# A decayed attention and gated convolution kernel on one core: its list of all engines' work, searched anew from cross4 on

## The chip, the cores and the metric

The kernel runs on one core of a Trainium2 chip. The metric is the device time of one execution in microseconds; of the kernel before three executions took 216.40, 216.54 and 216.66 us, so its time is the median, 216.54 us. Lower is better.

## What is computed

Two stages run one after the other on float32 data: a causal attention with a decay per head, in blocks of 64 positions with a running state, and then a gate from a convolution of five taps that multiplies a projected value, followed by an output projection.

```python
for b in range(nb):                      # 12 blocks of 64 positions, 4 batches, 8 heads of 64
    intra = (qb @ kb.T * Dmask) @ vb     # "scores", "mask", "cross"/"own"
    inter = (qb * lam_pow) @ kv_state    # "scale_q", "inter"
    out[:, :, sl] = intra + inter
    kv_state = lam_block * kv_state + (kb * rev_pow).T @ vb   # "scale_k", "outer", "update"
x = out.transpose(0, 2, 1, 3).reshape(4, 768, 512)
gate_pre = sum(conv_w[k] * x_padded[:, k:k + S] for k in range(5))   # "tap0" to "tap4"
gate = 1 / (1 + exp(-gate_pre))          # "sigmoid"
val = x @ w_val                          # "value"
return (gate * val) @ w_out              # "apply", "split_h", "project", "evict", "store"
```

The inputs w_val, conv_w and w_out arrive as float64 and are taken apart into float32 in the first 30 us; this part is not touched by the change.

## The kernel before, in words

The twelve blocks are the unit of work, i = 0 to 11. For each block the plan in `decay_attention_then_gated_conv` adds named steps, each of one engine. On TensorE a block has six kinds: `scores` (64 small matmuls of 64x64 blocks, line 469), `outer` (64, line 500), `cross` and `own` (32 each, line 535), `inter` (64, line 548), then two `value-i-u-` (24 matmuls of 128x128 with 256 columns, line 722) and two `project-i-b` (12 matmuls with 512 columns, line 789; the last block's second half is cut in two). Every matmul is a pair of instructions, a weight load and the multiplication. The first five kinds use the array as four blocks of 64x64 and are called small here; `value` and `project` use all of it and are called large.

VectorE has `mask`, `update`, `tap1` to `tap4` (line 659), `apply`, and `split_x_lo` of blocks 0, 5, 8, 11. ScalarE has `tap0`, `sigmoid`, `change`, `keep`, `split_x` (lines 602 and 606), `split_h`, `evict` (line 797) and the `scale_k` of eight blocks. GpSimd has `scale_q` (two a block, line 446), the other `scale_k`, `split_x_lo` (line 617) and `split_h_lo` (line 766). SyncE's queue issues all loads `ld` (q and k as four DMAs under `ldi-q0`; `ldi-v` and `ldi-k` two each; 256 KB a DMA, line 333) and all 25 stores (line 800), in the order in which they are named.

Numbers count as follows: `value-i-0-` and `value-i-2-` are the halves of block i; `apply`, `split_h` and `split_h_lo` count on over halves, so that numbers 2i and 2i+1 are those of block i; `scale_q` has none for block 0 and two for each block after it, so scale_q20 and scale_q21 are those of block 11.

What runs when is set by the list ORDER (line 39) alone: 600 names. `Plan.run` walks through it and issues each step's instructions, so each engine's queue is the list's names of that engine in the list's order. An engine takes its queue strictly in order and waits at the first step whose inputs or buffers are not there. Buffers come from SLOTS: three for the loads of a block (`ld`), two banks of PSUM for `scores`, `outer` and the accumulator of `cross`, `own` and `inter` (`d`), three for `value` and `project` (`u`), one for the taps (`acc`), two for outgoing rows (`o`). The code checks that the list respects dependencies and that a buffer is free when it is taken; the numbers of nanoseconds beside each step are not used when the list is walked.

Of the kernel before, what the change touches and what calls it, by code (L numbers as in the profile page):

```python
# [36 lines left out]


ORDER = """
qdec0 dmask0 go0 parts1 float_low1 mask_m1 add_low1 go1 parts2 relu1 sign1 scale1 mask_m2 ld0-q0 relu2  # L40
float_low2 add_low2 scores0 sign2 scale2 high1 mask0 low1 high0 low0 ld0-q1 scores1 mask1 ld1-q0 scores2
scale_q0 ld0-k scale_k0 ld0-v cross0 load_conv0 change0 mask2 parts0 go2 parts3 relu0 sign0 go3 mask_m3 parts4
float_low0 relu3 sign3 float_low3 add_low3 scale_q1 history0 mask_m0 mask_m4 add_low0 outer0 update0 own0
split_x0 scale3 ld1-v cross1 split_x_lo0 change1 own1 high2 low2 relu4 sign4 inter0 value-0-2 ld1-k keep0 go5
parts6 float_low4 scale0 ld2-q0 scores3 keep1 tap0-0-0 scale_q2 scale_q3 scale_k1 outer1 ld2-v add_low4 mask_m6
value-0-0 scale4 high3 split_x1 low3 value-0-3 ld2-k ld3-q0 history1 split_x_lo1 relu6 tap1-0-0 tap2-0-0
tap3-0-0 scale_q4 mask3 tap4-0-0 sigmoid-0-0 update1 value-0-1 tap0-0-1 tap1-0-1 scale_q5 float_low6 float_m0
go4 tap2-0-1 tap3-0-1 tap4-0-1 scores4 mask4 sigmoid-0-1 apply0 cross2 value-1-0 tap0-0-2 tap1-0-2 change2 own2
ld4-k add_low6 scale_k2 parts5 relu5 ld3-k float_low5 ld3-v tap2-0-2 sign6 value-1-1 mask_m5 inter1 keep2
split_x2 split_x_lo2 scale6 tap3-0-2 add_low5 high5 tap4-0-2 sigmoid-0-2 outer2 value-1-2 low5 update2 cross3  # L50
change3 tap0-0-3 ld5-q0 value-1-3 own3 tap1-0-3 inter2 apply2 keep3 tap2-0-3 tap3-0-3 scale_k3 sign5 value-2-0-
split_h2 tap4-0-3 sigmoid-0-3 scale5 split_h_lo2 high4 tap0-1-3 apply3 split_h3 outer3 low4 ld4-q0 scores5 ld7-v
apply1 mask5 value-2-2- split_h_lo3 split_h1 tap1-1-3 scores6 tap2-1-3 tap3-1-3 tap4-1-3 split_h0 mask6 scale_k4
sigmoid-1-3 tap0-1-0 project-1-1 evict-1-1 update3 split_h_lo1 split_h_lo0 ld4-v ld5-v cross4 scale_q6 outer4
ld5-k split_x3 change4 tap1-1-0 tap2-1-0 tap3-1-0 project-0-1 tap4-1-0 scale_q7 scale_q8 update4 sigmoid-1-0
inter3 own4 ld7-k history2 split_x_lo3 tap0-1-1 evict-0-1 store-0-1 cross5 scale_q9 tap1-1-1 tap2-1-1 tap3-1-1
tap4-1-1 change5 sigmoid-1-1 apply4 tap0-1-2 project-1-0 evict-1-0 tap1-1-2 tap2-1-2 own5 ld6-v store-1-0 inter4
keep5 split_x5 tap3-1-2 ld6-q0 tap4-1-2 sigmoid-1-2 apply5 ld7-q0 keep4 value-3-2- apply7 tap0-2-2 tap1-2-2
tap2-2-2 scale_k5 split_h4 split_h_lo4 scale_q10 value-3-0- apply6 scale_q11 split_h5 split_h_lo5 tap3-2-2
scale_k7 tap4-2-2 sigmoid-2-2 project-0-0 split_x_lo5 tap0-2-1 tap1-2-1 ld6-k history3 scores7 outer5 mask7  # L60
update5 split_h6 split_h_lo6 split_h7 project-2-0 evict-2-0 split_x4 split_x_lo4 tap2-2-1 project-2-1 ld8-q0
cross6 store-1-1 evict-0-0 tap3-2-1 tap4-2-1 sigmoid-2-1 store-0-0 store-2-0 scores8 mask8 evict-2-1 change6
store-2-1 tap0-2-3 tap1-2-3 scale_k6 tap2-2-3 scale_q12 scale_q13 value-5-2- value-4-2- ld8-k tap3-2-3 scale_k8
split_h_lo7 project-3-1 outer6 inter5 tap4-2-3 sigmoid-2-3 apply9 own6 split_h9 update6 tap0-2-0 value-4-0-
apply11 tap1-2-0 tap2-2-0 tap3-2-0 scale_q14 scale_q15 tap4-2-0 project-3-0 keep6 ld10-q0 sigmoid-2-0 evict-3-1
cross7 change7 apply8 split_h8 split_h_lo8 split_h_lo9 split_x6 outer7 split_h11 split_h_lo11 own7 inter6
value-5-0- keep7 ld9-k tap0-3-1 scale_k9 ld8-v store-3-1 tap1-3-1 tap2-3-1 ld9-q0 tap3-3-1 tap4-3-1 sigmoid-3-1
scores9 apply10 tap0-3-0 mask9 project-4-1 evict-4-1 store-4-1 split_x_lo6 update7 tap1-3-0 tap2-3-0 tap3-3-0
tap4-3-0 evict-3-0 split_h10 ld10-v store-3-0 sigmoid-3-0 split_x7 tap0-3-2 tap1-3-2 value-6-2- cross8 scores10
split_h_lo10 scale_q16 project-5-0 history4 evict-5-0 mask10 tap2-3-2 tap3-3-2 change8 value-6-0- apply12  # L70
tap4-3-2 sigmoid-3-2 inter7 own8 outer8 project-4-0 tap0-3-3 tap1-3-3 update8 tap2-3-3 split_x_lo7 ld9-v ld10-k
value-7-2- cross9 split_x8 split_x_lo8 keep8 scores11 change9 own9 tap3-3-3 tap4-3-3 sigmoid-3-3 split_h12
apply13 split_h13 ld11-q0 scale_q17 store-5-0 scale_q18 inter8 keep9 tap0-4-1 tap1-4-1 evict-4-0 store-4-0
tap2-4-1 project-5-1 apply15 tap3-4-1 mask11 evict-5-1 tap4-4-1 store-5-1 value-7-0- sigmoid-4-1 outer9 split_x9
apply14 split_h14 cross10 change10 split_h15 history5 split_h_lo12 split_h_lo13 scale_q19 project-6-1 evict-6-1
store-6-1 tap0-4-2 update9 value-8-0- tap1-4-2 tap2-4-2 tap3-4-2 scale_q20 scale_k10 split_h_lo15 split_h_lo14
project-7-0 evict-7-0 project-7-1 tap4-4-2 sigmoid-4-2 inter9 tap0-4-0 ld11-v store-7-0 evict-7-1 tap1-4-0
tap2-4-0 tap3-4-0 outer10 update10 split_x_lo9 value-9-0- tap4-4-0 sigmoid-4-0 apply16 apply18 tap0-4-3
scale_q21 tap1-4-3 value-8-2- scores12 project-6-0 tap2-4-3 tap3-4-3 value-9-2- mask12 tap4-4-3 split_h18
store-7-1 sigmoid-4-3 split_h16 split_h_lo16 apply17 split_h_lo18 split_h17 cross11 change11 own10 keep10  # L80
inter10 own11 evict-6-0 store-6-0 split_h_lo17 keep11 tap2-5-3 tap0-5-1 apply19 tap1-5-1 project-8-0 project-8-1
split_h19 split_h_lo19 tap1-5-3 project-9-0 tap2-5-1 tap3-5-1 tap4-5-1 split_x11 split_x_lo11 split_x10
sigmoid-5-1 evict-8-1 evict-8-0 tap0-5-0 tap1-5-0 tap0-5-3 tap2-5-0 tap3-5-0 tap4-5-0 sigmoid-5-0 store-8-0
tap0-5-2 tap1-5-2 evict-9-0 tap3-5-3 split_x_lo10 join1-5-3 join2-5-3 join3-5-3 value-11-2- value-11-0-
store-8-1 store-9-0 tap2-5-2 tap3-5-2 tap4-5-3 join4-5-3 project-9-1 apply22 split_h22 evict-9-1 value-10-2-
value-10-0- split_h_lo22 tap4-5-2 sigmoid-5-3 sigmoid-5-2 apply23 split_h23 split_h_lo23 apply21 project-11-1-1
split_h21 split_h_lo21 apply20 split_h20 store-9-1 evict-11-1-1 split_h_lo20 project-11-0 evict-11-0 store-11-0
project-10-1 evict-10-1 store-11-1-1 store-10-1 project-10-0 project-11-1-0 evict-10-0 store-10-0 evict-11-1-0
store-11-1-0
""".split()  # L90


# [760 lines left out]
```

## Time and profile before

| | us |
|---|---|
| three executions | 216.40, 216.54, 216.66 |
| the profiled execution, its own time | 218.14 |
| its span, first to last instruction | 216.4 |
| TensorE busy in the span | 199.0 |
| VectorE, ScalarE, GpSimd busy | 143.5, 114.1, 101.6 |

The profiled execution took 218.14 us, of which 216.4 us lie between its first and last instruction; without the profiler the whole execution takes 216.54 us. A gap on TensorE that the profile puts down to "issue" is one in which no semaphore that the profile shows was waited for. The rows that the prediction uses stand in the section before it.

### The profile page before, as it was taken

The numbers are of one execution on the slowest core, as the hardware profiler recorded it, in microseconds if no ns is written. First come the engines' busy times: TensorE is split into PE (matmuls) and PEld (weight loads), VectorE is DVE, ScalarE is ACT, GpSimd is POOL, SyncE is SP. The second block draws the span as 40 slices with busy tenths as digits, with TensorE's granted clock in tenths as the row PEclk, the third lists the DMA queues.
The fourth block names the chain that finished last, engine by engine and source line by source line (L and its number), as shares of the span: only waits on it lengthen the run. The fifth ranks groups of instructions, "written<-read, shape, count | busy, mean of one in ns | idle before, by whom it ended". The sixth has DMA issues, their size and how long they took to land.

```text
span 216.4 us, 8533 instructions
## 1 busy us (share of the span) xinstructions
PE 199.0 (92%) x3832; PEld 175.1 (81%) x3832; DVE 143.5 (66%) x220; ACT 114.1 (53%) x193; POOL 101.6 (47%) x81
## 2 busy tenths in 40 slices
PE   8838659999997899999799998999999999999993
PEld 3437659999986698798689988899889998899983
DVE  2998998999999649725923956919448832774100
ACT  3326876886853394237437642363741239855221
POOL 1171469155999209690409175018650052655600
PEclk9976978999999999999999999999999999999999
DMA  6999999157681396734155991612141001211022
GB/s 228 352 386 387 384 353 306 53 151 245 204 286 53 101 289 252 220 123 145 37 162 164 314 301 59 177 72 100 53 138 57 5 0 55 85 60 48 3 103 91
DMA packets 19188, 35.70 MB, mean 165 GB/s; under 512 B 2384, under 2 KB 2640, under 8 KB 19152
## 3 DMA queue, kind: packets, MB, share of 16 engines
q1 hardware_dynamic: 19008, 35.16, 47.9%
q8 instruction: 30, 0.49, 1.0%
q14 instruction: 6, 0.05, 0.1%
q10 hardware_dynamic: 144, 0.00, 0.0%
HBM read 28.86 MB, written 6.29 MB: 162 GB/s over the span
## 4 chain that ended last, share of the span: by engine, by line
PE 83%; DMA 7%; DVE 6%; issue 3%; SPq 1%; ACT 0%; DVEq 0%; ACTq 0%
PE op L789 32%; PE vp L722 31%; PE xp L535 5%; PE st L500 5%; PE xp L548 5%; PE s L469 4%; DMA w_raw<-in_w_out 3%; DMA w_raw<-in_w_val 2%; DMA lam_bc<-in_lam 2%; DVE w_m L276 1%; DVE w_e L267 1%; DVE w_m L250 1%; DVE w_m L283 1%; DVE w_e L244 1%; SPq L364 1%
## 5 line engine op out<-in xcount | busy, mean ns | idle before, releaser
L659 DVE SCALAR_TENSOR_TENSOR acc<-x,conv_sb,acc 128x512 f32<-128x512 f32 x92 | 69.3, 753 | 31.4 <-ACT acc L654 29.5
L789 PE MATMUL op<-wo_hi,hs 128*128 128x512 f32 (+1 forms) x200 | 61.2, 388 | 0.3 <-issue 0.3
L722 PE MATMUL vp<-x_hi,wv_hi 128*128 128x256 f32 x192 | 55.1, 287 | 0.0
L766 POOL TENSOR_TENSOR hs<-g,hs 128x512 fp32r<-128x512 f32 x24 | 31.4, 1326 | 48.8 <-ACT hs L763 48.8
L722 PE MATMUL vp<-x_lo,wv_hi 128*128 128x256 f32 x192 | 53.7, 280 | 0.0
L722 PE MATMUL vp<-x_hi,wv_lo 128*128 128x256 f32 x192 | 53.6, 279 | 0.0
L789 PEld LDWEIGHTS op<-wo_hi,hs 128*128 128x128 f32 x200 | 35.7, 188 | 7.2
L446 POOL TENSOR_TENSOR qd<-ld,qdec 128x512 f32<-128x512 f32 x22 | 29.0, 1335 | 24.9 <-DMA ld<-in_qkv 15.9
L789 PE MATMUL op<-wo_lo,hs 128*128 128x512 f32 (+1 forms) x100 | 38.4, 384 | 0.0
L722 PEld LDWEIGHTS vp<-x_hi,wv_hi 128*128 128x128 f32 x192 | 36.5, 190 | 1.3
L722 PEld LDWEIGHTS vp<-x_lo,wv_hi 128*128 128x128 f32 x192 | 36.4, 190 | 0.3
L722 PEld LDWEIGHTS vp<-x_hi,wv_lo 128*128 128x128 f32 x192 | 36.5, 190 | 0.0
L676 ACT ACTIVATE g<-acc 128x512 f32<-128x512 f32 x23 | 13.7, 598 | 29.3 <-DVE acc L659 29.3
L735 DVE TENSOR_TENSOR g<-vp,g 128x512 f32<-128x512 f32 x24 | 16.2, 687 | 18.1 <-ACT g L676 12.4
L797 ACT COPY o<-op 128x512 f32<-128x512 f32 (+1 forms) x25 | 14.0, 569 | 25.7 <-PE op L789 19.8
L617 POOL TENSOR_TENSOR x_lo<-x,x_hi 128x1024 fp32r<-128x1024 f32 x8 | 19.9, 2493 | 11.3 <-ACT x_hi L606 8.4
L789 PEld LDWEIGHTS op<-wo_lo,hs 128*128 128x128 f32 x100 | 18.8, 188 | 4.2 <-issue 0.5
L535 PE MATMUL xp<-A,ld 64*64 64x64 f32 x768 | 17.2, 228 | 4.9 <-issue 3.1
L535 PEld LDWEIGHTS xp<-A,ld 64*64 64x64 f32 x768 | 14.4, 141 | 7.8 <-issue 4.8
L763 ACT CAST hs<-g 128x512 fp32r<-128x512 f32 x24 | 14.3, 617 | 6.7 <-DVE g L735 6.3
L500 PE MATMUL st<-ld 64*64 64x64 f32 x704 | 14.8, 236 | 3.0 <-ACT wv_hi L288 2.2
L469 PE MATMUL s<-ld 64*64 64x64 f32 x768 | 14.6, 228 | 3.2 <-DVE A L477 3.2
(56 smaller groups left out, 229.9 us busy)
## 6 DMA issues: line engine op xcount, KB each, us to landing
ld<-in_qkv SPq DMA_DIRECT2D x90, 256.0 KB, 5.3
out<-o SPq DMA_DIRECT2D x23, 256.0 KB, 2.1
w_raw<-in_w_out SPq DMA_DIRECT2D x8, 256.0 KB, 5.9
w_raw<-in_w_val SPq DMA_DIRECT2D x2, 512.0 KB, 3.9
ld<-in_qkv SPq DMA_DIRECT2D x2, 512.0 KB, 6.6
w_raw<-in_w_val SPq DMA_DIRECT2D x4, 256.0 KB, 4.8
out<-o SPq DMA_DIRECT2D x2, 128.0 KB, 1.9
conv_raw<-in_conv_w SPq DMA_DIRECT2D x1, 20.0 KB, 4.9
```

The lines of the kernel that those rows point to most:

```text
L446: nc.gpsimd.tensor_tensor(out=s["qd"][:, p], in0=lds[i]["qT"][:, p], in1=qdec[:, :, p][:, :, None, :].to_broadcast([P, 2, NB, L]), op=ALU. ...
L469: nc.tensor.matmul(s["s", n][half(a), z, p, b], kT[half(z), p, a, b], qT[half(z), p, a, b], start=True, stop=True, skip_group_check=True,)
L500: nc.tensor.matmul(s["st"][half(z), a, p, b], k_[half(a), p, z, b], v_[half(a), p, z, b], start=True, stop=True, skip_group_check=True,)
L535: nc.tensor.matmul(s["xp"][half(p), z, a, b], lds[i]["v"][half(a), p, z, b], s["A"][half(a), z, p, b], start=t == 1 and b == 0, stop=True, ...
L617: nc.gpsimd.tensor_tensor(out=s["x_lo"].rearrange("q g b i -> q (g b) i"), in0=s["x"].rearrange("q g b i -> q (g b) i"), in1=hi.rearrange( ...
L659: nc.vector.scalar_tensor_tensor(out=to, in0=source(kk), scalar=w, in1=to, op0=ALU.mult, op1=ALU.add)
L722: nc.tensor.matmul(s["vp", u][:, f, :], w[:, ct, fs], xx[:, ct, :], start=n_mm == 0, stop=n_mm == 3 * NT - 1,)
L735: nc.vector.tensor_tensor(out=gs(u), in0=val, in1=gs(u), op=ALU.mult)
L763: nc.scalar.copy(s["h_hi"][:, us], gs(u))
L766: (nc.vector if i in H_DVE else nc.gpsimd).tensor_tensor(out=s["h_lo"][:, us], in0=gs(u), in1=s["h_hi"][:, us].bitcast(F32), op=ALU.subtract,)
L789: nc.tensor.matmul(op[:, cols], hh[:, ft, ts], w[:, ft, cols], start=n_mm == 0, stop=n_mm == 3 * NT - 1,)
L797: nc.scalar.copy(s["o", b, j][:, cols], s["op", b, j][:, cols])
```

## The change

Only the string ORDER differs. Its text is broken into lines anew, so that the diff shows all of it, but the first 205 names (up to `ld4-v ld5-v tap1-1-0`) are the same and stand in the same order. From there on the other 395 names stand in a new order; none is added or removed, and no other line of the kernel changes. The search that made the new list counted the semaphore waits of TensorE among the instructions of its program packets, and had the loads land later; neither figure is in the kernel.

The old list from `cross4` on (its first eleven lines), and the new one in full from the line in which it departs:

```diff
 ORDER = """
...
-sigmoid-1-3 tap0-1-0 project-1-1 evict-1-1 update3 split_h_lo1 split_h_lo0 ld4-v ld5-v cross4 scale_q6 outer4
-ld5-k split_x3 change4 tap1-1-0 tap2-1-0 tap3-1-0 project-0-1 tap4-1-0 scale_q7 scale_q8 update4 sigmoid-1-0
-inter3 own4 ld7-k history2 split_x_lo3 tap0-1-1 evict-0-1 store-0-1 cross5 scale_q9 tap1-1-1 tap2-1-1 tap3-1-1
-tap4-1-1 change5 sigmoid-1-1 apply4 tap0-1-2 project-1-0 evict-1-0 tap1-1-2 tap2-1-2 own5 ld6-v store-1-0 inter4
-keep5 split_x5 tap3-1-2 ld6-q0 tap4-1-2 sigmoid-1-2 apply5 ld7-q0 keep4 value-3-2- apply7 tap0-2-2 tap1-2-2
-tap2-2-2 scale_k5 split_h4 split_h_lo4 scale_q10 value-3-0- apply6 scale_q11 split_h5 split_h_lo5 tap3-2-2
-scale_k7 tap4-2-2 sigmoid-2-2 project-0-0 split_x_lo5 tap0-2-1 tap1-2-1 ld6-k history3 scores7 outer5 mask7
-update5 split_h6 split_h_lo6 split_h7 project-2-0 evict-2-0 split_x4 split_x_lo4 tap2-2-1 project-2-1 ld8-q0
-cross6 store-1-1 evict-0-0 tap3-2-1 tap4-2-1 sigmoid-2-1 store-0-0 store-2-0 scores8 mask8 evict-2-1 change6
-store-2-1 tap0-2-3 tap1-2-3 scale_k6 tap2-2-3 scale_q12 scale_q13 value-5-2- value-4-2- ld8-k tap3-2-3 scale_k8
-split_h_lo7 project-3-1 outer6 inter5 tap4-2-3 sigmoid-2-3 apply9 own6 split_h9 update6 tap0-2-0 value-4-0-
...
+split_h_lo1 split_h_lo0 ld4-v ld5-v tap1-1-0 scale_q6 scale_q7 scale_q8 split_x3 outer4 project-0-1 history2
+evict-0-1 tap2-1-0 tap3-1-0 update4 cross4 ld5-k tap4-1-0 sigmoid-1-0 cross5 project-1-0 tap0-1-1 tap1-1-1 tap2-1-1
+change4 inter3 change5 own5 scale_q9 store-0-1 own4 tap3-1-1 evict-1-0 store-1-0 tap4-1-1 sigmoid-1-1 apply4
+tap0-1-2 tap1-1-2 split_h4 tap2-1-2 ld6-q0 split_x_lo3 inter4 tap3-1-2 project-0-0 tap4-1-2 keep5 keep4 evict-0-0
+split_x5 split_x_lo5 ld6-k store-1-1 sigmoid-1-2 split_h_lo4 ld6-v tap0-2-2 tap1-2-2 tap2-2-2 apply5 tap3-2-2
+value-3-2- apply7 split_h5 tap4-2-2 sigmoid-2-2 value-3-0- scale_k5 outer5 apply6 split_h_lo5 scores7 project-2-0
+store-0-0 mask7 tap0-2-1 tap1-2-1 tap2-2-1 scale_k6 project-2-1 tap3-2-1 tap4-2-1 update5 ld7-k evict-2-0 split_x4
+ld7-q0 split_x_lo4 sigmoid-2-1 split_h7 scores8 mask8 ld8-v cross6 change6 split_h_lo7 value-5-2- outer6 tap0-2-3
+tap1-2-3 tap2-2-3 tap3-2-3 tap4-2-3 scale_q10 scale_q11 own6 evict-2-1 store-2-1 split_h6 ld9-k ld9-q0 sigmoid-2-3
+inter5 keep6 tap0-2-0 tap1-2-0 apply11 tap2-2-0 ld8-k split_h_lo6 project-3-1 store-2-0 history3 scale_q12
+scale_q13 value-4-2- apply9 split_h9 tap3-2-0 tap4-2-0 sigmoid-2-0 scale_k7 value-4-0- update6 apply8 project-3-0
+split_x6 split_x_lo6 cross7 change7 evict-3-1 split_h11 split_h_lo9 split_h_lo11 evict-3-0 split_h8 ld8-q0
+scale_q14 outer7 update7 own7 inter6 ld10-v keep7 tap0-3-1 value-5-0- tap1-3-1 tap2-3-1 tap3-3-1 tap4-3-1
+sigmoid-3-1 value-6-0- apply10 split_h_lo8 split_h10 tap0-3-0 tap1-3-0 tap2-3-0 tap3-3-0 tap4-3-0 scale_k8 ld10-q0
+scale_q15 history4 project-4-1 scores9 mask9 sigmoid-3-0 apply12 outer8 update8 value-6-2- split_x7 store-3-1
+tap0-3-2 cross8 split_h_lo10 scale_q16 tap1-3-2 scale_k9 scores10 tap2-3-2 tap3-3-2 tap4-3-2 mask10 change8 inter7
+sigmoid-3-2 project-5-0 store-3-0 ld9-v evict-5-0 store-5-0 evict-4-1 tap0-3-3 tap1-3-3 own8 keep8 cross9 change9
+split_x8 ld10-k split_x_lo7 split_x_lo8 tap2-3-3 tap3-3-3 project-4-0 tap4-3-3 sigmoid-3-3 apply13 value-7-2-
+scale_q17 inter8 own9 scores11 keep9 history5 split_h13 split_h12 split_h_lo12 apply15 split_h_lo13 evict-4-0
+scale_k10 store-4-0 project-5-1 value-7-0- store-4-1 apply14 tap0-4-1 mask11 tap1-4-1 tap2-4-1 scale_q18 scale_q19
+tap3-4-1 tap4-4-1 project-6-0 split_h14 evict-6-0 split_h15 store-6-0 sigmoid-4-1 outer9 update9 tap0-4-2
+project-6-1 outer10 cross10 evict-6-1 tap1-4-2 ld11-q0 tap2-4-2 evict-5-1 tap3-4-2 tap4-4-2 sigmoid-4-2 update10
+split_h_lo14 split_h_lo15 project-7-1 project-7-0 store-6-1 change10 tap0-4-0 tap1-4-0 split_x9 tap2-4-0 tap3-4-0
+evict-7-1 scores12 scale_q20 mask12 store-5-1 inter9 ld11-v tap4-4-0 sigmoid-4-0 tap0-4-3 evict-7-0 split_x_lo9
+value-9-0- apply18 split_h18 tap1-4-3 scale_q21 split_h_lo18 value-8-0- apply16 value-8-2- tap2-4-3 split_h16
+split_h_lo16 value-9-2- cross11 tap3-4-3 tap4-4-3 sigmoid-4-3 apply17 split_h17 split_h_lo17 change11 own10 own11
+store-7-0 store-7-1 inter10 apply19 keep10 project-8-0 project-8-1 keep11 tap2-5-3 tap0-5-1 tap4-5-3 split_h19
+tap1-5-1 tap1-5-3 split_h_lo19 project-9-1 evict-8-0 store-8-0 tap0-5-3 join1-5-3 join2-5-3 tap2-5-1 split_x11
+tap3-5-1 project-9-0 evict-8-1 tap4-5-1 sigmoid-5-1 tap0-5-0 tap1-5-0 tap3-5-3 split_x10 split_x_lo11 value-11-0-
+tap2-5-0 tap3-5-0 store-8-1 tap4-5-0 sigmoid-5-0 evict-9-1 apply22 tap0-5-2 tap1-5-2 value-11-2- tap2-5-2
+split_x_lo10 join3-5-3 join4-5-3 sigmoid-5-3 split_h22 split_h_lo22 evict-9-0 tap3-5-2 tap4-5-2 sigmoid-5-2 apply23
+value-10-0- apply20 split_h23 store-9-0 store-9-1 value-10-2- apply21 split_h_lo23 project-11-1-1 split_h20
+split_h_lo20 split_h21 split_h_lo21 evict-11-1-1 store-11-1-1 project-11-0 evict-11-0 store-11-0 project-10-1
+evict-10-1 store-10-1 project-10-0 evict-10-0 store-10-0 project-11-1-0 evict-11-1-0 store-11-1-0
 """.split()
```

TensorE's queue from the point of departure, before and after (names cut to kind and number: s scores, o outer, c cross, w own, i inter, v value, p project):

```
before c4 o4 p01 i3 w4 c5 p10 w5 i4 v32 v30 p00 s7 o5 p20 p21 c6 s8 v52 v42 p31 o6 i5 w6 v40 p30 c7 o7 w7 i6 v50 s9 p41 v62
       c8 s10 p50 v60 i7 w8 o8 p40 v72 c9 s11 w9 i8 p51 v70 o9 c10 p61 v80 p70 p71 i9 o10 v90 v82 s12 p60 v92 c11 w10 i10 w11
       p80 p81 p90 v112 v110 p91 v102 v100 p1111 p110 p101 p100 p1110
after  o4 p01 c4 c5 p10 i3 w5 w4 i4 p00 v32 v30 o5 s7 p20 p21 s8 c6 v52 o6 w6 i5 p31 v42 v40 p30 c7 o7 w7 i6 v50 v60 p41 s9 o8
       v62 c8 s10 i7 p50 w8 c9 p40 v72 i8 w9 s11 p51 v70 p60 o9 p61 o10 c10 p71 p70 s12 i9 v90 v80 v82 v92 c11 w10 w11 i10
       p80 p81 p91 p90 v110 v112 v100 v102 p1111 p110 p101 p100 p1110
```

`scores` count one ahead of their block, since block 0 has two.

## Rows read from the trace of the kernel before

**Rows 1.** The page: engines' busy time and instructions; TensorE's program packets (count, MB).

```profile
PE 199.0 (92%) x3832; PEld 175.1 (81%) x3832; DVE 143.5 (66%) x220; ACT 114.1 (53%) x193; POOL 101.6 (47%) x81
...
q8 instruction: 30, 0.49, 1.0%
```

**Rows 2.** Busy time by engine, 62.4 to 213.1 us; then granted clock, DMA share, GB/s.

```profile
62.40:213.10 150.70, 146.61 (x2577) 130.98 (x2576) 87.59 (x130) 73.26 (x126) 68.96 (x54) 1.00 0.36 119
```

**Rows 3.** Waits of TensorE, 62.4 to 216.4: line, cause, us, times, longest.

```profile
PE xp L535 <- issue: 3.1, 2, 1.6
```

**Rows 4.** The chain that ended last, around four gaps: start, us, what.

```profile
64.04 2.50 PE op L789 x10
66.53 0.30 issue
66.83 0.62 PE op L789 x2
67.46 1.09 PE xp L548 x64
68.55 0.92 PE xp L535 x61
69.47 1.62 issue
71.09 0.33 PE xp L535 x3
...
104.50 1.46 issue
...
133.65 0.81 PE st L500 x53
134.46 0.71 issue
135.17 0.45 PE st L500 x11
```

**Rows 5.** The same chain: the same kinds of work in different neighbourhoods.

```profile
113.54 0.47 PE xp L535 x32
...
114.94 2.93 PE vp L722 x24
...
118.96 2.96 PE op L789 x12
121.93 2.83 PE vp L722 x24
...
193.93 2.75 PE op L789 x12
196.67 5.47 PE vp L722 x48
```

**Rows 6.** DMA from 103 to 104.5 us: program packets.

```profile
q8 instruction: 1, 0.02, 5.1%
```

**Rows 7.** DMA from 75.4 to 82 us: program packets, loads (median us to landing).

```profile
q8 instruction: 1, 0.02, 0.9%
...
ld<-in_qkv SPq DMA_DIRECT2D x10, 256.0 KB, 5.8
```

**Rows 8.** SyncE's issues in order of time.

```profile
69.49 0.90 SPq L333 DMA_DIRECT2D ld<-in_qkv  x2
```

**Rows 9.** Groups of instructions, 62.4 to 213.1 us: busy us, mean ns; idle before them.

```profile
L766 POOL TENSOR_TENSOR hs<-g,hs 128x512 fp32r<-128x512 f32 x20 | 25.5, 1290 | 46.5 <-ACT hs L763 46.5
...
L446 POOL TENSOR_TENSOR qd<-ld,qdec 128x512 f32<-128x512 f32 x16 | 20.4, 1293 | 8.9 <-issue 8.9
...
L617 POOL TENSOR_TENSOR x_lo<-x,x_hi 128x1024 fp32r<-128x1024 f32 x6 | 14.4, 2403 | 4.1 <-DMA ld<-in_qkv 1.7 <-DMA out<-o 1.3 <-ACT x_hi L606 1.2
...
L797 ACT COPY o<-op 128x512 f32<-128x512 f32 (+1 forms) x24 | 13.6, 577 | 24.8 <-PE op L789 19.0 <-DMA out<-o 4.6 <-issue 1.2
...
L606 ACT CAST x_hi<-x 128x1024 fp32r<-128x1024 f32 x6 | 6.3, 1044 | 0.0
```

More of the change, by code (lines that the diff above doesn't have):

```diff
@@ L39 @@
 ORDER = """
[L40 to L53, printed above, removed]
-sigmoid-1-3 tap0-1-0 project-1-1 evict-1-1 update3 split_h_lo1 split_h_lo0 ld4-v ld5-v cross4 scale_q6 outer4
@@ L65 @@
[L65 to L89, printed above, removed]
+qdec0 dmask0 go0 parts1 float_low1 mask_m1 add_low1 go1 parts2 relu1 sign1 scale1 mask_m2 ld0-q0 relu2 float_low2
@@ new lines @@
+add_low2 scores0 sign2 scale2 high1 mask0 low1 high0 low0 ld0-q1 scores1 mask1 ld1-q0 scores2 scale_q0 ld0-k
+scale_k0 ld0-v cross0 load_conv0 change0 mask2 parts0 go2 parts3 relu0 sign0 go3 mask_m3 parts4 float_low0 relu3
+sign3 float_low3 add_low3 scale_q1 history0 mask_m0 mask_m4 add_low0 outer0 update0 own0 split_x0 scale3 ld1-v
+cross1 split_x_lo0 change1 own1 high2 low2 relu4 sign4 inter0 value-0-2 ld1-k keep0 go5 parts6 float_low4 scale0
+ld2-q0 scores3 keep1 tap0-0-0 scale_q2 scale_q3 scale_k1 outer1 ld2-v add_low4 mask_m6 value-0-0 scale4 high3
@@ new lines @@
+split_x1 low3 value-0-3 ld2-k ld3-q0 history1 split_x_lo1 relu6 tap1-0-0 tap2-0-0 tap3-0-0 scale_q4 mask3 tap4-0-0
+sigmoid-0-0 update1 value-0-1 tap0-0-1 tap1-0-1 scale_q5 float_low6 float_m0 go4 tap2-0-1 tap3-0-1 tap4-0-1 scores4
+mask4 sigmoid-0-1 apply0 cross2 value-1-0 tap0-0-2 tap1-0-2 change2 own2 ld4-k add_low6 scale_k2 parts5 relu5 ld3-k
+float_low5 ld3-v tap2-0-2 sign6 value-1-1 mask_m5 inter1 keep2 split_x2 split_x_lo2 scale6 tap3-0-2 add_low5 high5
+tap4-0-2 sigmoid-0-2 outer2 value-1-2 low5 update2 cross3 change3 tap0-0-3 ld5-q0 value-1-3 own3 tap1-0-3 inter2
@@ new lines @@
+apply2 keep3 tap2-0-3 tap3-0-3 scale_k3 sign5 value-2-0- split_h2 tap4-0-3 sigmoid-0-3 scale5 split_h_lo2 high4
+tap0-1-3 apply3 split_h3 outer3 low4 ld4-q0 scores5 ld7-v apply1 mask5 value-2-2- split_h_lo3 split_h1 tap1-1-3
+scores6 tap2-1-3 tap3-1-3 tap4-1-3 split_h0 mask6 scale_k4 sigmoid-1-3 tap0-1-0 project-1-1 evict-1-1 update3
+split_h_lo1 split_h_lo0 ld4-v ld5-v tap1-1-0 scale_q6 scale_q7 scale_q8 split_x3 outer4 project-0-1 history2
+evict-0-1 tap2-1-0 tap3-1-0 update4 cross4 ld5-k tap4-1-0 sigmoid-1-0 cross5 project-1-0 tap0-1-1 tap1-1-1 tap2-1-1
```

## The prediction, made before the changed kernel was run

> **What bounds the kernel now.** I read the busy times first: TensorE works 199.0 of the 216.4 us of the span [rows 1]. Then the same by stage, because the list departs only at cross4, at about 62.4 us: from 62.4 to 213.1 us TensorE is busy for 146.61 of 150.70 us at a granted clock of 1.00, while VectorE, ScalarE and GpSimd need 87.59, 73.26 and 68.96 [rows 2]. So the stretch lasts as long as TensorE's own work plus its gaps, and the gaps are 4.09 us. Third, what ended them: the view of TensorE's waits has three lines for this stretch, all with the cause "issue"; the largest is shown [rows 3], the other two are the 0.30 and the 0.71 of the chain. No gap is put down to another engine or to a load. Last, the chain shows where they lie: 0.30, 1.62, 1.46 and 0.71 us, the last three in the midst of a run of small matmuls [rows 4].
>
> What ends an "issue" gap? Between the first and the second lie 2 + 64 + 61 = 127 matmuls [rows 4], which with their weight loads are 254 instructions. All of TensorE's 3832 pairs, 7664 instructions, came in 30 program packets [rows 1], 255 a packet without its waits. A gap thus stands where one packet is used up and the next has not come. I read it so: a packet is asked for when the one before it begins to be used, and TensorE stops when it uses 256 instructions faster than the next packet can come. A packet's worth of small matmuls takes little: 32 take 0.47 us [rows 5], so 128 take 1.9 us. In the window before the gap of 1.46 us, one program packet is all there is on the DMA queues [rows 6], and yet TensorE had to wait.
>
> **How long a packet takes**, from the begin of the one before it to the end of the gap. Second gap: 66.83 to 71.09, 4.3 us. Third: the 127 small pairs before it took 1.9 us, so 1.9 + 1.46 = 3.4 us. Fourth: 1.9 + 0.71 = 2.6 us. First, with loads in flight: the packet before it holds 10 matmuls of project-0-1 (2.50 [rows 4]), 64 of outer4 and 32 of cross4 (1.4 + 0.16 [rows 5]) and ahead of them project-1-1 (2.96 [rows 5]) and some 10 of scores6 (0.15): 7.2 us, and with the gap 7.5 us. So 2.6 to 4.3 us with the queues quiet, up to about 7.5 us behind loads.
>
> The Trainium skill, page "Runtime: NRT & Kernel Launch", section "Instruction fetch mechanics", says that the program comes in blocks of 256 instructions, that the next is fetched while the current one runs, and that crossing a block is mostly hidden. The block's size agrees with rows 1 and 4; that it is hidden does not hold for runs of small matmuls, where rows 4 have 4.09 us. By the page's rule the gaps would have another cause and would stay, and the sum would be 216.2 us; that is a rival below.
>
> **The change, part by part.**
>
> *The packets.* I laid the new list's TensorE work end to end, with prices from rows 5: 0.47 for 32 small, 0.155 more where a small run follows a large one (1.09 for 64 against 2 x 0.47), 2.96 and 2.75 for a project after small and after large work, 2.93, 2.83 and 2.73 (half of 5.47) for a value after small, project and value. Counting 256 instructions each, and spreading the waits evenly over the small groups, the packets from 62.5 us on last, in the old list, 2.2, 6.6, 7.7, 7.4, 9.5, 1.9, 7.2, 4.4, 7.4, 7.2, 2.0 and then never under 5; and the three short ones are those before the last three gaps, which is the check of the reading. In the new list they last 4.8, 5.2, 6.4, 7.4, 4.6, 7.0, 7.1, 4.5, 6.9, 4.6, 4.8, 7.3, 5.2, 9.4, 7.4, 4.8, 8.9, 7.5, 17.3. The first, as a sample: cross5 0.47, project-1-0 2.96, inter3 1.09, own5's first 18 matmuls 0.26. The small runs are cut by a project each time (cross4 and cross5, then project-1-0, where the old list had inter3, own4 and cross5 in a row). A few waits more or fewer move the shortest by 0.2. None is under 4.3 us: the three long gaps go, and the first too, since its boundary moves from the middle of project-0-1 to the end of cross4, 0.4 us later by TensorE's work, more than the gap.
>
> What goes with a gap is more than its idle time, because a run that is cut starts again: own4 and cross5 took 0.92 + 0.33 against 2 x 0.47, 0.31 more; outer8 0.81 + 0.45 against 0.94, 0.32 more; I take the same for the third cut run; project-0-1 took 2.50 + 0.62 against 2.96, 0.16 more [rows 4, 5]. Sum: 4.09 + 0.31 + 0.32 + 0.32 + 0.16 = 5.2 us.
>
> *Kinds of neighbours.* Counted over both lists: large to small 15 times in both; small to project 10, now 11 (+0.21); small to value 5, now 4 (-0.20); project to value 8, now 5 (-0.30). Sum -0.3 us.
>
> *Loads and stores.* On SyncE's queue loads move against each other and past stores. An issue costs 0.45 us [rows 8] and lands 5.8 us later in a burst [rows 7]; a store's issue I take at the same. ld6-v, first of block 6 before, is now behind ld6-q0, ld6-k and store-1-1; all wait for own4 to free the buffer, at 72.6 on the laid-out clock, and scores7 starts at 83.1: 4 x 0.45 + 5.8 leaves 2.9 us. ld7-k and ld7-q0 come 14 issues and two stores after 72.6, so land by 85.6, before scores8 at 89.8. ld9-k, ld9-q0 and store-2-0 now stand around ld8-k and ld8-q0, which land by 108, with scores9 at 119.4. ld10-k, now behind store-5-0, lands by 137.5, with outer10 at 151.8. ld11-q0 is the closest: it stands behind store-6-0, so behind evict-6-0 and project-6-0, which ends at 147.7: 0.58 [rows 9] + 0.45 + 1.8 + 5.8 is 156.3; scores12 needs it at 159.0, and on GpSimd scale_q20 (1.29) and split_x_lo9 (2.40) [rows 9] follow it, 160.0 against value-9-0 at 161.0. One us to spare. So cost 0, and each us by which it is later than that is a us of TensorE.
>
> *GpSimd and ScalarE.* scale_q10 and scale_q11, scale_k6, k8, k9 and k10 move. The closest: after project-2-0 (end 87.0) come evict-2-0 0.58 and split_x4 1.04, then on GpSimd split_x_lo4 2.40, split_h_lo7, scale_q10, scale_q11 and split_h_lo6 at 1.29: 96.2, and project-3-1 wants the last at 96.7 [rows 9]. Half a us to spare; in the old list scale_q10 and q11 were ahead of this. That sum takes the queue to be empty ahead of it, so I price this part at 0 to 1.5 us, below 0 not, since TensorE had no such wait to lose [rows 3], and take 0.2.
>
> *Packets behind loads.* The new packet of 6.4 us lies in the burst of ld6 and ld7, two of 6.9 and 7.1 near the loads of blocks 8 to 10. At 7.5 us a packet they would be short by 1.1, 0.6 and 0.4. Against it: in the old burst, 75.4 to 82, a packet came among ten loads [rows 7] and no gap followed [rows 3, 4]. Between 0 and 2.1 us; I take 0.1, nearer to the row of the same kind.
>
> **The sum.** 216.4 - 5.2 - 0.3 + 0.2 + 0.1 = 211.2 us of span. Without the profiler the whole execution takes 216.54, 0.1 more than the profile's span (its own 218.14 has the profiler around it), so I carry the difference over: 211.3 us.
>
> **Rivals.**
> - *Some packets come late behind loads, or a chain on GpSimd is late by one step.* One packet at the worst price, or one link late by a GpSimd step of 1.3 us: 211.7 to 213.6, say 212.6. For it: slack of 0.5 and 1.0 us. Against: TensorE had no data wait with queues as full.
> - *The change doesn't do what it says*: the gaps are not of the packets and come again elsewhere. Only the -0.3 stays: 216.2. Against: 127 matmuls between gaps, and three short packets at three gaps. The Trainium skill's sentence above would have it so.
> - *Slower: a packet asked for during a burst comes only after the whole burst.* The new list issues ld6 and ld7 in one (14 loads and two stores from 72.6: 16 x 0.45 + 5.8, landed at 85.6), and with 2.6 us for the packet TensorE would go on at 88.2 instead of 83.4: 4.8. Blocks 8 and 9 (from 95.8: 12 loads, one store, landed at 107.5, packet 110.1 against 109.5): 0.6. Block 10 (from 110.1: eight loads, two stores, landed at 120.4, packet 123.0 against 120.9): 2.1. Sum 7.5, so 218.8. It decides from 5.3 us on. Against: rows 7, a packet among the loads.
>
> **Chances.** Forecast 0.55 (210.8 to 211.8), late packet or link 0.24, no effect 0.08, slower 0.06; between these, with half of the gain lost, 0.07. A difference under about 0.2% cannot be told from none here. Faster 0.86, same 0.08, slower 0.06. Range 210.7 to 213.8: it leaves out the no-effect and slower cases and most of the half-lost one, 0.2 in all; its upper end holds one of the two unknown costs at its worst (1.3 or 2.0 more than taken) and half a microsecond of the other.
>
> **What would show it.** Right: no "issue" gap over 0.2 us after 62 us, the chain nearly all TensorE to the end and the same tail of project, evict and store. Wrong: "issue" gaps at other runs of small matmuls, above all between 80 and 88 or 119 and 124 (packets behind loads); a gap at project-3-1 ended by GpSimd's split_h_lo6 (line 766), or at value-9-0 or scores12 ended by a load.

## The result, and the profile after

The new list takes 213.72 us (median of four executions, 212.80 to 214.85) against 216.47 us (216.40 to 216.66) for the kernel before on the same chip. The ratio is 0.9869, its interval 0.9825 to 0.9913. The forecast was 211.3 us with a range of 210.7 to 213.8: the direction held, and the time lies at the range's upper end. The gain is 2.75 us where 5.2 was predicted.

In the page of the kernel after, the span and busy times answer to [rows 1]; line numbers are two lower than before.

```profile
span 211.0 us, 8536 instructions
PE 197.1 (93%) x3832; PEld 173.0 (82%) x3832; DVE 144.0 (68%) x220; ACT 114.0 (54%) x193; POOL 101.8 (48%) x81
q8 instruction: 30, 0.49, 1.0%
```

The stretch from the end of project-1-1 to the last matmul answers to [rows 2]: length, then busy time of TensorE, its weight loads, VectorE, ScalarE and GpSimd, granted clock, DMA share, GB/s.

```profile
61.99:207.76 145.77, 145.77 (x2577) 130.34 (x2576) 87.58 (x130) 73.40 (x126) 68.94 (x54) 1.00 0.37 122
```

TensorE is busy for the whole of its 145.77 us, where before it was busy for 146.61 of 150.70. The view of TensorE's waits from 62 to 208 us, which answers to [rows 3], has no line left in it. The chain of waits shows the place of the first two gaps of [rows 4] in the new order (start, us, what):

```profile
61.99 1.09 PE st L498 x64
63.09 2.97 PE op L787 x12
66.06 1.09 PE xp L533 x64
67.15 2.95 PE op L787 x12
70.10 1.09 PE xp L546 x64
71.19 0.93 PE xp L533 x64
72.13 0.93 PE xp L546 x64
73.06 2.97 PE op L787 x12
76.03 3.98 PE vp L720 x35
```

Each small run is short or holds no packet that is used up quickly, and none is cut. Profile against profile the span fell from 216.4 to 211.0 us, by 5.4, and 4.9 of that lie in this stretch. (The other 0.5 is the start: project-1-1 ends at 61.99 instead of 62.48, although the list is the same up to there. It ended anywhere from 61.99 to 63.30 in the profiles in which nothing was added ahead of scores0.) So the forecast of the span, 211.2, was met by the profile, and yet the executions differ by only 2.75 us. (The profiled execution took 212.80 us, the shortest of the four, and that of the kernel before 218.14, longer than any of its others.) That discrepancy, and whether the gaps are really those of program packets, is what the experiments are about.

### The profile page after: what moved, and what is told of

It reads as the page before. It is cut to its first block, busy times and chain, and to the rows that moved or that the text cites. A ratio compares the mean times of both kernels' runs of the same rounds, so it can differ in the third digit from the quotient of the medians.

```text
span 211.0 us, 8536 instructions
## 1 busy us (share of the span) xinstructions
PE 197.1 (93%) x3832; PEld 173.0 (82%) x3832; DVE 144.0 (68%) x220; ACT 114.0 (54%) x193; POOL 101.8 (48%) x81
## 4 chain that ended last, share of the span: by engine, by line
PE 80%; DMA 11%; DVE 6%; ACT 1%; issue 1%; SPq 0%; DVEq 0%; ACTq 0%
PE op L787 33%; PE vp L720 29%; PE xp L533 5%; PE xp L546 5%; PE st L498 4%; DMA ld<-in_qkv 4%; PE s L467 4%; DMA w_raw<-in_w_out 3%; DVE acc L657 3%; DMA w_raw<-in_w_val 2%; DMA lam_bc<-in_lam 2%; DVE w_m L274 1%; DVE w_m L248 1%; DVE state L510 1%; DVE A L475 1%
## 5 line engine op out<-in xcount | busy, mean ns | idle before, releaser
L720 PEld LDWEIGHTS vp<-x_hi,wv_hi 128*128 128x128 f32 x192 | 36.0, 188 | 1.0
L533 PE MATMUL xp<-A,ld 64*64 64x64 f32 x768 | 15.8, 226 | 3.1 <-DVE A L475 1.5
L510 DVE SCALAR_TENSOR_TENSOR state<-state,qdec,st 128x256 f32<-128x256 f32 x40 | 16.5, 473 | 2.9 <-PE st L498 2.9
L467 PEld LDWEIGHTS s<-ld 64*64 64x64 f32 x768 | 13.3, 142 | 6.0 <-DVE A L475 3.1
```

The source lines that it names most:

```text
L467: nc.tensor.matmul(s["s", n][half(a), z, p, b], kT[half(z), p, a, b], qT[half(z), p, a, b], start=True, stop=True, skip_group_check=True,)
L510: nc.vector.scalar_tensor_tensor(out=new[:, a, p], in0=s["state"][:, a, p], scalar=qdec[:, a, p, L - 1 : L], in1=s["st"][:, a, p], op0=ALU ...
L533: nc.tensor.matmul(s["xp"][half(p), z, a, b], lds[i]["v"][half(a), p, z, b], s["A"][half(a), z, p, b], start=t == 1 and b == 0, stop=True, ...
L720: nc.tensor.matmul(s["vp", u][:, f, :], w[:, ct, fs], xx[:, ct, :], start=n_mm == 0, stop=n_mm == 3 * NT - 1,)
```

## The experiments

Two theories. **P**: a gap stands where a border between two program packets falls into work that uses a packet up before the next one is usable, so that it moves with the count of instructions. **W**: a gap belongs to a place in the work (own6 after project-3-1, outer8 after inter7), whatever its count. A "stretch" is below always that from the end of project-1-1 to the end of the last matmul.

**The same two kernels once more.** No edit.

> The new list once more, for the size of the gain and for a second profile. The profile of before (span 216.4) was 1.6 us longer in its own time (218.14) than the plain executions of the same kernel (216.5), while the profile of the new list (span 211.0, own time 212.8) is the shortest of its four executions (212.8 to 214.85). Theory P: the program-packet gaps after 62 us are gone for good, and the median of 213.7 instead of 211.3 comes from executions that differ before 62 us. It expects 213 to 214.5 us and no issue gap over 0.2 us after 62 us in this profile too. Rival W: the new list has gaps after 62 us in most executions, and its first profile had luck. It expects a second profile with 1 to 3 us of gaps there.

> The old list once more, unchanged, for a second profile. If the first profile was a long execution because of what lies before 62 us, this one reaches cross4 earlier than 62.4 us by up to 1.6 us and has the same four gaps (0.3, 1.6, 1.5, 0.7 us) after it. If instead the gaps themselves vary, the gaps sum to about 2.5 us here instead of 4.1, at the same places. Time 216.5 us.

The new list again: 213.42 us (beside 215.95 for the kernel before), ratio 0.9884 (0.9845 to 0.9924); no gap, stretch 145.98 us (columns as in [rows 2]):

```profile
62.06:208.04 145.98, 145.98 (x2577) 130.57 (x2576) 87.49 (x129) 73.30 (x126) 68.74 (x54) 1.00 0.37 122
```

The old list again: 216.26 us, ratio 1.0008 (0.9972 to 1.0044). But its profile is not the one that I predicted from. Its span is 213.4 us, 3.0 less than [rows 1] had, and of the four gaps of [rows 4] two are there. TensorE's waits from 62.4 us, then the chain around the larger one, then the stretch:

```profile
PE xp L535 <- issue: 1.2, 1, 1.2
PE st L500 <- issue: 0.5, 1, 0.5
```

```profile
96.78 2.75 PE op L789 x12
99.53 1.09 PE st L500 x64
100.62 0.93 PE xp L548 x64
101.56 0.46 PE xp L535 x28
102.02 1.19 issue
103.21 0.33 PE xp L535 x4
```

```profile
62.37:210.17 147.80, 146.07 (x2577) 130.72 (x2576) 87.42 (x130) 73.35 (x126) 68.58 (x54) 1.00 0.37 122
```

The third and fourth gap of [rows 4] stand in both executions, at the same matmuls. The first two, 0.30 and 1.62 us, don't. The DMA view shows what differed. By the count of instructions that is explained below, the border ahead of the packet whose coming ended the first gap lies at 59.2 us, amid loads. In the first profile, the whole of 59.2 to 64.0 us shows no program packet, with the engines nearly full of loads (queue, kind: packets, MB, share):

```profile
q1 hardware_dynamic: 867, 1.57, 95.4%
```

In the second the same packet is on the queues between 61.6 and 63.2 us, among the loads:

```profile
q1 hardware_dynamic: 226, 0.41, 86.1%
q8 instruction: 1, 0.02, 5.1%
```

So in the first execution it came some 2.5 us later (its transfer began at 64.34, against 61.80), and the next one was late in turn. The two early gaps stand in one of the two executions, behind a packet that came late amid loads; the two late ones stand in both. Why loads let the packet through in one execution and not in the other is not shown.

**Shift the old and the new list against the packets.** The work stays in order, and small matmuls (64x64, on zeros) are added after the warm-up, so that everything behind them moves on against the packet borders. Each such line is four instructions.

```diff
+    for _ in range(108):          # old list; 40 in the new list
+        nc.tensor.matmul(warm[0:L, 0, 0:L], zero[0:L, 0:L], zero[0:L, 0:L], start=True, stop=True, skip_group_check=True)
```

> The old list with 108 more small matmuls of zeros into the warm-up bank ahead of all work, 216 instructions: every boundary of a program packet moves by 216 instructions against the work, and nothing else changes after 10 us. Counted on the trace of before, no packet after 55 us then lasts under 3.6 us. Theory P: all four gaps after 62 us go with the order of work unchanged; the time from cross4 to the last matmul falls from 150.6 to about 145.7 us, the execution to about 213 us, if the added work costs nothing at the start, where TensorE waits for its first load until 9.0 us. Rival D, that the gaps come from the order of loads, stores and other engines in the old list: the gaps stay, 216.5 us.

> The new list with 40 more small matmuls of zeros at the start, 80 instructions. Counted on its trace, six packets then last 1.9 us, used up at about 73, 96, 110, 126, 138 and 174 us. Theory P: six gaps there of 0.7 to 2.4 us each (a packet took 2.6 to 4.3 us in the old list), 7 to 12 us in all: 221 to 226 us, slower than before. Rival D: nothing changes, 213.7 us.

I had counted the added instructions at half of what they are: the shifts were 432 (176 past a full packet) and 160. They also weren't free, since TensorE already fills the time up to scores0: scores0 began at 21.46 and 13.32 us instead of 9.0, so 222.26 us (ratio 1.0305, 1.0253 to 1.0357) and 219.08 us (1.0157, 1.0117 to 1.0198) say nothing on the gaps; the profiles do. TensorE's waits in the stretch, the old list shifted (the added lines move its line numbers up by two):

```profile
PE st L502 <- issue: 1.5, 1, 1.5
```

and the new list shifted:

```profile
PE op L789 <- issue: 0.8, 1, 0.8
PE xp L548 <- issue: 0.4, 1, 0.4
```

The old list has no gap any more at own6 and outer8, but one at outer5; the new list, which had none, has two. That is P's side. But I had expected six gaps and 7 to 12 us for the new list, and none for the old one; and by the true shifts three packets of the old list (2.1 to 3.1 us) and four of the new one (2.1 to 3.3 us) are short: not every packet that is used up quickly gaps. What decides is worked out below, after the last runs.

**Shift without adding work.** Wide warm-up matmuls (four instructions each too) are replaced by small ones. The old list is moved on by 204 instructions to where no packet after 62 us is used up quickly, the new list by 40 to where several are, and by 216 to where none is.

```diff
-WARM, WARM_END = 6, 5700.0
+WARM, WARM_END = 1, 5700.0        # new list moved by 40: 5
...
+    for _ in range(56):            # new list moved by 40: 11, by 216: 59
+        nc.tensor.matmul(warm[0:L, 0, 0:L], zero[0:L, 0:L], zero[0:L, 0:L], start=True, stop=True, skip_group_check=True)
```

> The old list unchanged, with five of the six wide warm-up matmuls (1.34 us each, four instructions) replaced by 56 small ones (0.122 us each, four instructions): the same 6.7 us of warm-up, but TensorE's work lies 204 instructions later against the borders of its program packets. Theory P (a packet border inside a run of small matmuls, with a packet that is used up in under some 2.8 us): counted over the profile of the old list no packet after 62 us is then used in under 4 us, so no issue gap there; from a typical execution of the old list (gaps of 1.2 and 0.5 and two cut runs at 0.3) that takes 2.3 us: 214.0 us, and the stretch from the end of project-1-1 to the last matmul about 145.4. Rival W (the gaps belong to the place in the work: own6 after project-3-1, outer8 after inter7): gaps of 1.2 to 1.5 and 0.5 to 0.7 there as before, 216.3 us, stretch 147.8.

> The new list with one wide warm-up matmul replaced by eleven small ones: the same warm-up time, TensorE's work 40 instructions later against the packet borders. Theory P: the packets that are then used fastest are at 71 us (1.9 us), 109 (2.5), 137 (1.9), 159 (2.5) and 172 (3.0) of the new profile; by the gaps seen so far 1 to 2 us at 71, 0.5 to 1 at 109 and at 137, 0 to 0.3 at the other two: 2 to 4 us in all with the restarts, 215.5 to 217.5 us. Rival W: the new list has no such places, so no gap, 213.5 us.

> The new list with five wide warm-up matmuls replaced by 59 small ones (the shift is 216 instructions). Theory P: no packet after 62 us is used in under 4 us, so no gap, and the time of the new list, 213.5 us within 0.7. It is also the control for the warm-up: if replacing wide matmuls by small ones costs time or clock by itself, it shows here, as a start of the stretch later than 62.0 us; then 214 to 217 us with no gap after it.

The old list at 204: its stretch has no gap and takes 145.49 us (145.4 expected), against 147.8 to 150.6 with gaps.

```profile
66.55:212.04 145.49, 145.49 (x2577) 130.43 (x2576) 87.67 (x130) 73.22 (x126) 69.07 (x54) 1.00 0.36 120
```

The new list at 216 has none either, 145.77 us. The new list at 40 has three, at 79.08, 118.28 and 147.05 us, where the packets of 1.9, 2.5 and 1.9 us were counted to be; the other two (2.5 and 3.0) made no gap, as the expectation allowed. Its waits in the stretch:

```profile
PE xp L548 <- issue: 1.4, 1, 1.4
PE s L469 <- issue: 1.2, 1, 1.2
PE vp L722 <- issue: 0.4, 1, 0.4
```

W is refuted: the same order with another count loses its gaps, and an order without gaps gets them. The time of the whole kernel again doesn't show it: 216.91 (ratio 1.0003, 0.9978 to 1.0029) for the old list at 204, 217.22 (1.0026, 0.9999 to 1.0053) for the new one at 216, since 56 lines of small matmuls on zeros took some 12 us at the start and not the 6.8 that I had worked out from the run before (40 lines in 4.8 us): scores0 began at 14.85 and 15.49 us, and the stretch 4.2 and 4.8 us after that of the repeated old list. The shift also moves the borders ahead of 62 us: TensorE's "issue" waits there come to 5.7 us in the old list at 204 and 7.0 in the new one at 216, against 1.2 in the repeated old list and 2.3 in the first profile of the new. How much of the later start is due to them is not shown. The new list at 40 scatters from 216.4 to 221.5 us (ratio 1.0045, 0.9987 to 1.0103), and only its profile is used here (an execution of 221.4 us; the granted clock of its stretch is 1.00, as in the others).

**Shift by taking work away.** All six warm-up matmuls go, in the old and in the new list: 24 instructions less, nothing added ahead of scores0.

```diff
-WARM, WARM_END = 6, 5700.0
+WARM, WARM_END = 0, 5700.0
```

> The old list with none of the six wide warm-up matmuls: TensorE's work lies 24 instructions earlier against its packet borders (the same as 232 later), and nothing is added ahead of scores0. Theory P: counted over the profile of the old list the fastest packet after 62 us is then one of 3.4 us at 133, and the others last over 4, so no issue gap over 0.2 there and a stretch from project-1-1 to the last matmul of 145.5, against 147.8 to 150.6 with the gaps. If the start is not hurt by the missing warm-up (the end of project-1-1 at 62 to 63 as in the profiles with 7 to 20 us at half clock), 214.0 us, as quick as the new list within 0.7. Rival W (the gaps belong to the order of the old list): two gaps of 1.2 to 1.5 and 0.5 to 0.7 remain, stretch 147.8, 216.4 us.

> The new list with none of the six warm-up matmuls: no packet after 62 us is then used in under 4 us, so no gap and a stretch of 145.8 as in the new list. The control for e9_old_nowarm: what the missing warm-up does to the start shows here alone. If the end of project-1-1 stays at 62 to 63, 213.5 us; each us later is a us more.

> The new list unchanged, beside the two kernels without the warm-up on the same chip: 213.5 us within 0.6, no issue gap after 62 us, stretch 145.8.

On one chip, where the kernel before took 216.51 us: the old list without warm-up 214.09 us (ratio 0.9880, 0.9833 to 0.9927), the new list without it 213.95 (0.9869, 0.9818 to 0.9920), the new list as it is 213.51 (0.9838, 0.9795 to 0.9882). **The old order, 24 instructions earlier, gains what the new order gains** within these intervals. Its gaps have not gone wholly:

```profile
PE op L789 <- issue: 0.5, 1, 0.5
PE vp L722 <- issue: 0.2, 1, 0.2
```

and its stretch is 146.57 us, where the two new lists on that chip have 145.27 with no gap. The missing warm-up costs the start little: project-1-1 ends at 61.99 and 63.30 us. Neither kernel beats the new list.

**One part alone: cut the two runs.** The old list with three steps moved, so that a project or a value stands inside each of the two runs with a lasting gap:

```diff
-split_h_lo7 project-3-1 outer6 inter5 ...
+split_h_lo7 outer6 project-3-1 inter5 ...
...
-... scale_q16 project-5-0 history4 evict-5-0 mask10 tap2-3-2 tap3-3-2 change8 value-6-0- apply12
-tap4-3-2 sigmoid-3-2 inter7 own8 outer8 project-4-0 ...
+... scale_q16 change8 project-5-0 history4 evict-5-0 mask10 tap2-3-2 tap3-3-2 inter7 value-6-0- apply12
+tap4-3-2 sigmoid-3-2 own8 outer8 project-4-0 ...
```

> The old list with two steps of TensorE moved and nothing else but one small copy of ScalarE: outer6 ahead of project-3-1 and inter7 ahead of value-6-0 (change8 ahead of evict-5-0), which cuts the two runs of 160 small matmuls that hold the two gaps that every profile of the old list has. Theory P: both gaps and their two cut runs go (1.73 + 0.6), and the new neighbours cost 0.155 + 0.21 + 0.155 + 0.1 and up to 0.2 of waiting for scale_k6: 2.3 - 0.7 = 1.6 us less than the old list, 214.7 us, stretch 146.2. Rival (what the new list gains lies in its order as a whole, on other engines and in loads, and not at these two places): gaps of the same size come elsewhere after 62 us, 216.3 us or more.

215.82 us, ratio 0.9961 (0.9932 to 0.9989): 0.8 us gained, half of the 1.6 expected. Both gaps are gone; what is there is the early one behind the loads, as in the first profile, and a wait for ScalarE's small copy ahead of scores11, which no other profile has. TensorE's waits in the stretch and the chain around the gap:

```profile
PE xp L535 <- issue: 1.3, 1, 1.3
PE s L469 <- ACT turn L541: 0.5, 1, 0.5
```

```profile
63.97 0.70 PE st L500 x48
64.67 3.09 PE op L789 x12
67.75 1.09 PE xp L548 x64
68.84 0.92 PE xp L535 x61
69.76 1.34 issue
```

Without gaps and wait the stretch of 148.91 is 147.1 us; against 145.49 that is 1.6 more, of which 0.6 are the new neighbours as priced and 0.3 a cut run. The other 0.7 I can't place.

**What decides whether a packet gaps.** Counting every instruction of TensorE's queue in the traces (weight loads, matmuls, semaphore waits), each "issue" gap of the stretches, in all of these kernels, stands 193 instructions past a multiple of 256 (within one instruction), for instance 4289 and 5569 in the old list, 3265, 4801 and 6081 in the new one moved by 40. The packets' own records give the second half (us; from the traces, some of them; "border before" and "used up" are the begin of a packet's last instruction, so the latter is some 0.2 us ahead of the end that the chain shows):

| kernel, gap | border before | transfer of the next packet | packet used up | TensorE goes on | after the transfer's end |
|---|---|---|---|---|---|
| before, third | 102.35 | 103.24 to 104.46 | 104.28 | 105.96 | 1.50 |
| old again, second | 129.57 | 129.86 to 130.79 | 131.48 | 132.24 | 1.45 |
| new at 40, first | 75.52 | 76.10 to 77.61 | 77.43 | 79.08 | 1.47 |
| new at 40, third | 143.76 | 144.39 to 145.63 | 145.67 | 147.05 | 1.42 |
| old at 176 (none) | 118.21 | 117.20 to 118.19 | 120.41 | 120.41 | 2.22 |
| new at 40 (none) | 167.13 | 165.77 to 166.72 | 169.66 | 169.67 | 2.95 |

In the gaps of all these profiles that end on a packet, TensorE went on 1.2 to 1.6 us after the packet's transfer had ended. In the last one of the new list at 40, nothing moves on any DMA queue while TensorE stands, from 145.7 to 147.0 us:

```profile
DMA packets 0, 0.00 MB, mean 0 GB/s; under 512 B 0, under 2 KB 0, under 8 KB 0
```

and the packet is the only transfer between 144.3 and 145.7 us:

```profile
DMA packets 1, 0.02 MB, mean 12 GB/s; under 512 B 0, under 2 KB 0, under 8 KB 0
q8 instruction: 1, 0.02, 5.5%
```

So at these gaps the next packet's transfer takes 0.9 to 1.5 us, then about 1.4 us pass, and there is a gap if the packet in use is used up before. When the transfer begins differs: 0.2 to 1.0 us after the border inside small runs with the queues quiet, 1.2 to 5.2 us where loads fill the queues, but up to 1.4 us ahead of it at some borders of short packets with large matmuls before them (up to 4.9 ahead at borders of long ones). That is why some short packets made no gap, and why I expected too many in the shifted lists. That TensorE's queue runs ahead of the array after slow matmuls, and so asks sooner, would explain the early ones; this is argued, not shown. Two transfers fit none of these: behind the first gap of the kernel before, and at the same border of the old list with the moved steps, the next packet began 1.8 and 1.2 us after the border with the queues nearly empty.

Counted over the stretches of all thirteen profiles, 19 packets were used up in under 3.1 us; 14 of them ended in a gap, of 0.2 to 1.6 us. In these 14 the next packet's transfer began 0.2 to 2.2 us after the border, in the five without a gap 0.3 to 1.4 us ahead of it. Of the longer ones one did, the first gap of the kernel before (7.4 us, behind loads).

## Why the prediction was half right

**What bounds, and the packets: right.** The gaps moved with the count of instructions and not with the work. The kernel is TensorE's own work in this stretch plus the gaps. None is left in the new list in any of its three profiles, nor in the two where it was shifted to other quiet counts.

**Whether a gap recurs: the step that failed.** The sum took four gaps, 4.09 us, and the cut runs beside them as the cost of every execution, and the text carried "the difference over" from the span, 216.4, to the time without the profiler, 216.54, as if the same execution stood behind both. It did not: in all these runs an execution's own time is its span and about 1.8 us, as 218.14 was to 216.4 and 212.80 to 211.0. So a span of 211.2 would have meant an execution of 213.0, and 216.54 belongs to a span of about 214.8: the profiled execution was a long one by 1.6 us. Two numbers of the table of times before, 218.14 and 216.54, were the warning. What the first profile had and the second of the old list had not were the first two gaps, priced at 0.30 + 0.16 and 1.62 + 0.31, 2.4 us of the 5.2, from a packet behind loads. The other two, priced at 1.46 + 0.31 + 0.71 + 0.32 = 2.8 us, stand in both (1.19 and 0.54 us in the second).

The measured gain is 2.75, 2.5 and 3.0 us in three comparisons. That this is near 2.8 proves no split. Profile against profile, the stretch of the new list is 4.9 us shorter than one of the old list with all four gaps, and 1.8 shorter (147.80 against 145.98) than one with the two late ones; the medians lie between, and the second profile of the old list is of one of its shorter executions (215.21 us, median 216.26). In how many executions the early gaps stand no run shows.

**Kinds of neighbours: not confirmed.** Predicted was -0.3 us. The old list without gaps has 145.49 us, the new one 145.27, 145.27, 145.77, 145.77 and 145.98: from 0.2 less to 0.5 more. So the gain doesn't come from the new neighbours; and TensorE waits for no other engine in the stretch, in the profiles of either list, so it doesn't come from there.

**Loads, GpSimd, packets behind loads: right at their size.** Taken were 0, 0.2 and 0.1 us; no wait for a load, GpSimd or a packet stands in the stretch of any profile of the new list. The links with 0.5 and 1.0 us to spare held.

**The rivals.** No effect: refuted. The sentence of the Trainium skill that crossing a block is mostly hidden ("Runtime: NRT & Kernel Launch", section "Instruction fetch mechanics") agrees with most borders here, but not with those of packets used up in under 3.1 us, where 14 of 19 cost 0.2 to 1.6 us. Late packet or link, 212.6: the median lies nearest to its figure, but its cause isn't there. Slower, a packet held up by the whole burst: not in the new list. Something like it stands in the first profile of the kernel before, though: one packet began 5.2 us after its border, when the burst had ebbed, and the early gaps followed; in the second profile the same packet came among the loads.

## What to carry to other kernels

Where TensorE runs many short instructions, count them (no other engine was tried): where a program packet's worth is used up in under some 3 us, the border of the packet can cost up to 1.6 us, and where the borders fall is set by the number of instructions ahead of them, so that a shift by a few dozen can be worth as much as a new order, as the 24 instructions here were. Before a gap is priced, look whether the profiled execution is a typical one (its own time against the other executions' times), and whether the gap has a cause that differs from run to run, as a transfer amid a burst of loads did here.

## What the runs showed of the hardware

- A program packet became usable 1.2 to 1.6 us after its transfer had ended, in every gap that ended on one, with the DMA queues empty as well as after loads.
- The transfer of one packet with its border amid loads began 5.2, 4.8 and 2.7 us after that border in three executions (the old list twice, and the one with the moved steps, which is the same up to there). The old list had 4.09 us of gaps in one execution and 1.73 in the other.
- The small matmuls of the stretch took 0.0146 us each (64 in 0.93 us), but 56 lines of those on zeros, 112 matmuls, took some 12 us behind one wide warm-up matmul, 0.108 each, and 40 lines behind the six wide ones 4.8 us, 0.06 each. The granted clock was 1.00 in both places. Those on zeros use one 64x64 block of the array and one output, unlike those of the stretch; whether that makes them slow was not tried.
- Dropping the warm-up matmuls, of some 8 us, moved the end of project-1-1 to 61.99 and 63.30 us, inside or near the range that it has with them.
